# A planned start: ranks of the flags behind the far V products, and other landing costs in the plan

## The chip, the cores and the metric

One core of a Trainium2 chip runs the whole kernel in one launch. The metric is the device time in microseconds, the median of several runs.

## The reference

The reference is causal attention over 4 batches, 8 heads, 768 positions and 64 channels, and then a two-layer map over all 3072 tokens. Some heads see all earlier positions ("retrieval" heads, by a flag per head that is an input), the others see the first 4 positions ("sinks") and a window of 64:

```python
scores = scale * np.matmul(q, k.transpose(0, 1, 3, 2))
mask = np.where(retr[0, :, 0, 0, None, None], causal, causal & (is_sink | in_win))
scores = np.where(mask, scores, -1e9)
a = np.exp(scores - max); a = a / (a.sum(-1) + 1e-09)
x = np.matmul(a, v)  # (B, S, H * D) = (3072, 512)
h = x @ w_in         # 512 -> 2048
out = (h - np.tanh(h)) @ w_out   # 2048 -> 512
```

## The kernel before

The 3072 tokens are 12 tiles of 256 (three to a batch). For each tile the kernel makes Q and K with the channels in the partitions (`QK`), takes scores for each pair of heads (`st_S`, matmuls of line 1063, exp of line 1076), multiplies the probabilities with V (`st_A`, line 1156), divides (`rinv`, line 1176), lays the result out for the next matmul (`x`, line 1203, `xT`, lines 951 and 1238) and runs the two layers: H units (line 1267, tanh of line 1279, `gt` of line 1286) and O groups (line 1325, out through line 1299).

Nothing is ordered by a loop alone. Each piece of work is an `op` of the class `Plan`: an engine, a cost in ns, the keys that it reads and writes, and a priority, which is its place in the program. `Plan.run` walks through time with these costs, gives each engine the ready op of lowest priority, and so writes out each engine's order; the instructions are then issued in that order. Keys are names for the plan: real data dependencies get their semaphores from the tiles, and a key that stands for no data only delays an op in the plan.

For a DMA the plan has a cost on the issuing engine, a number of packets, ns for each packet (a sixteenth of their product is the transfer), and a pair `lag`: time from the issue to the transfer's start and from its end to the landing. Transfers of one ring go one after the other; rings that are live share. On POOL at most 8 DMAs may be under way: the ninth waits, in the plan, for the first to be done (its end + 1.8 us), the tenth for the second, and so on; if another op of POOL is ready meanwhile, it goes first. An op marked `port` on DVE that the plan starts while POOL computes, or 0.35 us or more into a DMA issue on POOL, is stretched to that op's end.

At the start, Q and K of tile 0 are loaded on SP's queue. POOL's queue brings the rest: V of tile 0 in two blocks (`load_v`, line 490), Q and K of tile 1 packed (`t16p`, line 523), V of tile 1, w_in in four parts, w_out in four parts, V, Q and K of tile 2, and tile 3's raw Q, K and V (line 592). DVE casts `t16p` into order (`in_order`, line 542), PE turns it (line 968) and DVE copies it to `QK` (line 951). `scale_v` on POOL makes the far V products `vf` (line 725): V of key blocks 0 to 3 of batch 0, times the head's flag; each tile brings two blocks. `select` (line 736) makes the mask pieces `A4` and `mS`, and one copy (line 933) fills the last part of `mS`.

From batch 1 on, heads are taken in the order of their flags. `by_rank` computes that order from the flags by a chain of small DVE instructions (lines 841 to 908), then the masks `m4r` and `mS` (lines 917 to 933), and loads the ranks `perm_i` into registers of POOL and DVE (line 938); POOL's `gather` (line 636) of tile 3 uses them. The chain's instructions wait in the plan for the keys of `LATE`.

PE's idle stretches of the first 18 us are filled, as far as the plan sees them, with products of a matrix of ones (line 1482).

Of the kernel before, what the change touches and what calls it, by code (L numbers as in the profile page):

```python
# [12 lines left out]
TT = 256  # L13
# [242 lines left out]
def kernel(  # L256
# [90 lines left out]
    XE = ("DDDD", "DDDD")  # L347
    NAMED = {"A": "ACT", "D": "DVE"}
    SV = "POOL"
    FILLS = 30  # L350
    FILL_END = 18000.0
    CASTS = (('ACT', 'DVE'), ('DVE', 'ACT'))
# [1 line left out]
    GATE = {3: (1, 0), 4: (1, 1)}  # L354
    CUT1 = (-10.5,-6.0,2.25,13.5)
    FLEX = 2
    LEAD = 3
    QUART = 7
    LD = 22
# [1 line left out]
    FROM = 3  # L361
    BR = 1
    FRONT = "A40"
    LATE = [("x16", 3)]
    BEHIND = [("x16", 1)]
    MASKS = 2
    A2 = (4, 9)
    ORDER = ("t1", "v1", 0, 1, 2, 3, 4, "t2", 5, "r3", 6, 7)

    def program(first):  # L370

# [111 lines left out]
        def load_v(t):  # L483

            b, g = divmod(t, NG)
            for i in range(NB):
                blk = g * NB + i
                dma(
                    "POOL", 900,
                    lambda i=i, blk=blk: nc.gpsimd.dma_start(  # L490
                        out=v1s[b]()[:, blk, :, 0:D],
                        in_=v[b, :, blk * 128 : blk * 128 + 128, :].rearrange("h p d -> p h d"),
                    ),
                    128 * H, 15.5, w=[("v1", b, blk, x) for x in range(2)],
                )

        def load_cast(t):

            b, g = divmod(t, NG)
            batch(b)  # L500
            c, ic = t16s[t] = buf("t16")
            if t >= FROM:
                c5 = lambda: c()[:].rearrange("p (i x h d) -> p i x h d", i=NB, x=2, h=H)
                for i in range(NB):
                    s0 = g * TT + i * 128
                    for x, src in enumerate((q, k)):
                        dma(
                            "POOL", 900,
                            lambda i=i, x=x, src=src, s0=s0: nc.gpsimd.dma_start(
                                out=c5()[:, i, x, :, :],  # L510
                                in_=src[b, :, s0 : s0 + 128, :].rearrange("h p d -> p h d"),
                            ),
                            128 * H, 15.5, w=[("t16", ic, x, i, s_) for s_ in range(H)],
                        )
                load_v(t)
                for i in range(NB):
                    turn(t, i)
                return
            packed[t] = pk, ip = buf("t16p")
            for x, src in enumerate((q, k)):  # L520
                dma(
                    "POOL", 950,
                    lambda x=x, src=src: nc.gpsimd.dma_start(
                        out=pk()[:].rearrange("p (x h e) -> p x h e", x=2, h=H)[:, x, :, :],
                        in_=src[b, :, g * TT : (g + 1) * TT, :].rearrange(
                            "h (p i) d -> p h (i d)", i=2
                        ),
                    ),
                    128 * H, 22.6, w=[("t16p", ip, x)],
                )  # L530
            if t == 1 and first:
                return
            in_order(t)
            load_v(t)

        def in_order(t):

            (pk, ip), (c, ic) = packed[t], t16s[t]
            for x in range(2):
                op(  # L540
                    "DVE", 500,
                    lambda x=x: nc.vector.tensor_copy(
                        out=c()[:].rearrange("p (x i h d) -> p x i h d", x=2, i=2, h=H)[:, x],
                        in_=pk()[:].rearrange("p (x h i d) -> p x i h d", x=2, h=H, i=2)[:, x],
                    ),
                    r=[("t16p", ip, x)] + (BEHIND if t == 1 and first else []),
                    w=[("t16", ic, x, half) for half in range(2)], port=True,
                )

        def turn(t, i):  # L550

# [166 lines left out]
        def scale_v(t, eng="POOL"):  # L718
            b, g = divmod(t, NG)
            lo = g * NB  # L720
            for jb in range(lo, min(lo + NB, 4)):
                fl = rflag0 if jb == 0 else rflag
                op(
                    eng, {"DVE": 690, "POOL": 1053}[eng],
                    lambda jb=jb, fl=fl: engs[eng].tensor_mul(
                        out=vfs[b]()[:, jb, :, :], in0=v1s[b]()[:, jb, :, :],
                        in1=fl[:].unsqueeze(2).to_broadcast([128, H, D + 1]),
                    ),
                    r=[("v1", b, jb, 0), ("v1", b, jb, 1), "rflag0", "rflag"],
                    w=[("vf", b, jb, 0)], port=True,  # L730
                )

        def select(m, src, fill, base, step, mult, key, cmp=ALU.is_ge):
# [272 lines left out]

        def st_S(units):

            todo, reads, keys, ns = [], [], [], 160
            for n, gi in units:  # L1010
                t, hp = divmod(n, HP)
                b, g = divmod(t, NG)
# [329 lines left out]
        def visits(t):  # L1342
            g = t % NG
            gen = [t * HP + hp for hp in range(HP) if not is_near(t * HP + hp)]
            near = [t * HP + hp for hp in range(HP) if is_near(t * HP + hp)]
            if near:
                a, c = gen
                d, e = near
                return {
                    0: [[(a, 0), (d, 0)], [(c, 0), (e, 0)]],  # L1350
                    1: [[(a, 0), (a, 1)], [(d, 0), (c, 0)], [(c, 1), (e, 0)]],
                    2: [[(a, 0), (a, 1)], [(a, 2), (d, 0)], [(c, 0), (c, 1)], [(c, 2), (e, 0)]],
                }[g]
# [153 lines left out]
        def spread_over(fs, lo, hi):  # L1507
            for i, f in enumerate(fs):
                plan.setdefault(max(0, int(lo + (hi - lo) * i / max(len(fs), 1))), []).append(f)

        if first and fast:
            spread_over([by_rank], BR, BR)
        spread_over(att_pairs(1) + [lambda: scale_v(1, SV)], 0, 0)
        spread_over(attention(2), *A2)
        between = {}

# [115 lines left out]
```

## Time and profile before

| | us |
|---|---|
| median of 3 runs | 232.07 |
| lowest, highest | 231.43, 232.75 |
| profiled execution, its time | 233.06 |
| profiled execution, span of its instructions | 231.3 |
| PE busy in the span | 221.7 (96%) |
| DVE, ACT, POOL busy | 146.7, 139.9, 97.5 |

The time of an execution stands beside the span that the profiler saw on the core; what lies around the span is 1.8 us here. Rows of a timeline give start, duration, engine, line, operation, output and inputs, and in brackets how long the engine was idle before and what released it. Rows of a table by stretches give for each engine the busy time and the number of instructions, then the granted PE clock (1.00 is full), the DMA share and GB/s. Rows of waits give the total, the count and the longest.

### The profile page before, as it was taken

The page shows a single profiled execution, that of the slowest core. Times are in us where ns is not written, and L with a number is a line of the kernel's source. Part 1 is how long each engine was busy: PE and PEld are TensorE (multiplying, and loading weights), DVE is VectorE, ACT ScalarE, POOL GpSimd, SP SyncE. Part 2 cuts the span into 40 slices and gives each one's busy share as a digit, 9 for nine tenths or more (in the row PEclk, how much of TensorE's full clock was granted, in tenths as well). Part 3 has the DMA queues.
Part 4 walks back from the last instruction along what each step waited for, and adds up shares of the span by engine and source line. Part 5 has one row for each costly group of instructions (what it writes and reads, how often), then busy time and mean ns, then how long its engine had stood idle before and what let it go on. Part 6 is the DMA issues. An engine that isn't in the chain of part 4 may idle for free.

```text
span 231.3 us, 6135 instructions
## 1 busy us (share of the span) xinstructions
PE 221.7 (96%) x2328; PEld 158.7 (69%) x2328; DVE 146.7 (63%) x355; ACT 139.9 (60%) x214; POOL 97.5 (42%) x231
## 2 busy tenths in 40 slices
PE   7879999989999999999999999999999999999992
PEld 6446788768887666766776676765957767766652
DVE  5878887893774766755774776466867547534400
ACT  3817837975566858747547756846875867534420
POOL 8998361980281918684363968280000000000000
PEclk9988999999999999999999999999999999999999
DMA  6999999979999999999979999944121211220112
GB/s 171 150 194 206 186 223 217 208 114 204 198 202 233 195 197 233 206 198 209 248 149 252 222 250 185 212 117 114 48 45 48 60 34 45 67 47 28 48 63 80
DMA packets 102964, 35.31 MB, mean 153 GB/s; under 512 B 90642, under 2 KB 100114, under 8 KB 102930
## 3 DMA queue, kind: packets, MB, share of 16 engines
q1 hardware_dynamic: 85632, 27.14, 56.3%
q0 software_dynamic: 17152, 7.60, 25.1%
q8 instruction: 19, 0.31, 0.6%
q14 instruction: 15, 0.12, 0.2%
q10 hardware_dynamic: 146, 0.13, 0.2%
HBM read 27.26 MB, written 6.29 MB: 145 GB/s over the span
## 4 chain that ended last, share of the span: by engine, by line
PE 84%; DVE 6%; DMA 3%; POOL 2%; ACT 2%; issue 1%; POOLq 0%; DVEq 0%
PE banks L1325 36%; PE banks L1267 34%; PE banks L1063 7%; PE banks L1156 6%; DMA t16p<-in_k_dram 3%; DVE gt L1286 2%; DVE pt L1117 2%; ACT pt L1076 1%; DVE prod L846 1%; POOL v L490 1%; PE banks L968 1%; PE banks L1052 1%; ACT th L1279 1%; DVE QK L951 0%; POOL A L736 0%
## 5 line engine op out<-in xcount | busy, mean ns | idle before, releaser
L1267 PE MATMUL banks<-xT,win 128*128 128x256 f16 x768 | 95.0, 273 | 0.7 <-DVE gt L1286 0.5
L1325 PE MATMUL banks<-wout,gt 128*128 128x512 f16 (+1 forms) x464 | 94.5, 343 | 1.1 <-DVE gt L1286 1.1
L1286 DVE SCALAR_TENSOR_TENSOR gt<-th,banks 128x512 f16<-128x512 f32 x96 | 65.1, 682 | 31.5 <-ACT th L1279 30.7
L1267 PEld LDWEIGHTS <-win 128*128 128x128 f16 x768 | 72.8, 98 | 15.5 <-issue 2.1
L1279 ACT ACTIVATE th<-banks 128x512 f32<-128x512 f32 x96 | 57.1, 601 | 40.5 <-PE banks L1267 39.4
L1076 ACT ACTIVATE pt<-banks 128x768 f16<-128x768 f32 (+1 forms) x60 | 52.9, 920 | 17.3 <-PE banks L1063 16.4
L1325 PEld LDWEIGHTS <-gt 128*128 128x128 f16 x464 | 43.0, 98 | 29.3 <-DVE gt L1286 1.3
L636 POOL CAST t<-rawqk 128x256 f16 x72 | 28.6, 443 | 30.6 <-DMA rawqk<-in_k_dram 14.7
L1299 ACT ACTIVATE ot<-banks 128x512 f32<-128x512 f32 (+1 forms) x28 | 15.0, 535 | 22.0 <-PE banks L1325 21.2
L1188 DVE TENSOR_TENSOR x16t<-banks,rinv 128x128 f32 (+1 forms) x80 | 22.9, 288 | 1.8 <-DVE x16t L1188 0.2
L1099 DVE TENSOR_TENSOR ptn<-ptn,mS 128x512 f16<-128x512 f16 x24 | 10.9, 493 | 17.0 <-ACT ptn L1076 17.0
L1063 PE MATMUL banks<-QK 64*128 64x128 f16 (+1 forms) x364 | 21.4, 241 | 0.0
L672 POOL CAST v<-rawv 128x128 f16 x72 | 19.7, 320 | 0.0
L1063 PEld LDWEIGHTS <-QK 64*128 64x128 f16 x364 | 12.7, 95 | 9.9 <-issue 6.8
L1076 ACT ACTIVATE ptn<-banks 128x1024 f16<-128x1024 f32 (+1 forms) x18 | 17.2, 953 | 3.8 <-PE banks L1063 3.7
L1156 PEld LDWEIGHTS <-pt 128*128 128x128 f16 x420 | 16.3, 97 | 3.8 <-ACT pt L1076 0.7
L1156 PE MATMUL banks<-v,pt 128*128 128x65 f16 x220 | 16.6, 193 | 0.3 <-ACT pt L1076 0.2
L1127 DVE TENSOR_TENSOR pt<-pt,m4r 128x1024 f16<-128x1024 f16 (+1 forms) x18 | 12.4, 686 | 5.0 <-ACT pt L1076 5.0
L1176 DVE RECIPROCAL rinv<-banks 128x4 f32<-128x4 f32 x48 | 8.5, 177 | 8.5 <-PE banks L1156 7.7
L1156 PE MATMUL banks<-vf,pt 128*128 128x65 f16 x200 | 13.1, 193 | 0.0
L661 POOL COPY kc<-QK 128x128 f16<-128x128 f16 x12 | 3.5, 290 | 12.0 <-DMA QK<-t 11.9
L1156 PEld LDWEIGHTS <-ptn 128*128 128x128 f16 x132 | 6.4, 97 | 2.2
(79 smaller groups left out, 137.2 us busy)
## 6 DMA issues: line engine op xcount, KB each, us to landing
out_dram<-ot SPq DMA_DIRECT2D x19, 256.0 KB, 2.5
rawqk<-in_q_dram SPq DMA_DIRECT2D x18, 256.0 KB, 3.8
rawqk<-in_k_dram SPq DMA_DIRECT2D x18, 256.0 KB, 4.4
rawv<-in_v_dram SPq DMA_DIRECT2D x16, 256.0 KB, 4.6
win<-in_moe_w_in_dram POOLq DMA_DIRECT2D x4, 512.0 KB, 11.3
wout<-in_moe_w_out_dram POOLq DMA_DIRECT2D x4, 512.0 KB, 13.2
out_dram<-ot SPq DMA_DIRECT2D x9, 128.0 KB, 3.8
v<-in_v_dram POOLq DMA_DIRECT2D x6, 128.0 KB, 6.8
```

The lines of the kernel that those rows point to most:

```text
L636: nc.gpsimd.tensor_copy(out=c5()[:, :, :, s_ : s_ + 1, :], in_=r5()[:, :, :, at, :])
L672: nc.gpsimd.tensor_copy(out=v1s[b]()[:, g * NB : g * NB + NB, RANK[s_] : RANK[s_] + 1, 0:D], in_=rv()[:, :, at, :],)
L1063: nc.tensor.matmul(out=sc()[:, hh, o : o + nb * 128], lhsT=lhsT, rhs=QK[p_, hp, q_0 : q_0 + nb * 128], start=not added, stop=not added or ...
L1076: lambda pt=pt, sc=sc, gi=gi, wid=wid: nc.scalar.activation(out=pt()[:, :, 512 * gi : 512 * gi + wid], in_=sc()[:, :, 0:wid], func=AF.Exp, ...
L1127: nc.vector.tensor_mul(out=pv, in0=pv, in1=m)
L1156: nc.tensor.matmul(out=av()[:, i, hh, :], lhsT=pt()[:, hh, co : co + 128], rhs=vv, start=(jb == first_jb), stop=(jb == qb),)
L1188: nc.vector.tensor_mul(out=xt()[:, :, at, :], in0=av()[:, :, hh : hh + 1, 0:D], in1=rinv()[:, :, hh : hh + 1].unsqueeze(3).to_broadcast([1 ...
L1267: nc.tensor.matmul(out=ph()[:, j, :], lhsT=w_in_t[fb // 4][:, cb, f0 : f0 + 128], rhs=xT()[:, :, cb, :], start=(cb == 0), stop=(cb == HP - 1),
L1279: lambda: nc.scalar.activation(out=th()[:], in_=ph()[:], func=AF.Tanh, scale=1.0 / XS),
L1286: lambda: nc.vector.scalar_tensor_tensor(out=gt()[:, u * FU : (u + 1) * FU, :], in0=th()[:], scalar=-XS, in1=ph()[:], op0=ALU.mult, op1=AL ...
L1299: nc.scalar.activation(out=ot()[:, c0:c1], in_=po()[:, c0:c1], func=AF.Copy, scale=1.0 / XS)
L1325: nc.tensor.matmul(out=po()[:, c0:c1], lhsT=gt()[:, f, ts * 128 : ts * 128 + 128], rhs=w_out_t[:, f, c0:c1], start=(f == 0), stop=(f == NF ...
```

## The change

The ranks wait in the plan for the key ("vf", 0, 3, 0), which is the product of V's key block 3 of batch 0, in place of ("x16", 3), which is the fourth head pair of tile 0's attention output. The plan's numbers of the first loads change: ns for each packet of V of tiles 0 and 1 (15.5 to 17.5), of Q of tile 1 (22.6 to 37.0), the lag of the first V load (1100 to 1500), and the fixed part of a score visit's cost on PE (160 to 225). The other edits add choices that are set to what was there: `PARTS` 1, `TRI` empty, `SPLIT` beyond every slot, `SV1` equal to `SV`, and in `scale_v` a branch for ACT that is not taken.

```diff
--- before.py
+++ after.py
@@ -347,6 +347,7 @@
     XE = ("DDDD", "DDDD")
     NAMED = {"A": "ACT", "D": "DVE"}
     SV = "POOL"
+    SV1 = "POOL"
     FILLS = 30
     FILL_END = 18000.0
     CASTS = (('ACT', 'DVE'), ('DVE', 'ACT'))
@@ -354,6 +355,12 @@
     GATE = {3: (1, 0), 4: (1, 1)}
     CUT1 = (-10.5,-6.0,2.25,13.5)
     FLEX = 2
+    V1E = 17.5
+    V0LAG = 1500
+    Q1E = 37.0
+    PARTS = 1
+    TRI = ()
+    SPLIT = 1 << 30
     LEAD = 3
     QUART = 7
     LD = 22
@@ -361,11 +368,11 @@
     FROM = 3
     BR = 1
     FRONT = "A40"
-    LATE = [("x16", 3)]
+    LATE = [("vf",0,3,0)]
     BEHIND = [("x16", 1)]
     MASKS = 2
     A2 = (4, 9)
-    ORDER = ("t1", "v1", 0, 1, 2, 3, 4, "t2", 5, "r3", 6, 7)
+    ORDER = ("t1","v1",0,1,2,3,4,"t2",5,"r3",6,7)
 
     def program(first):
 
@@ -491,7 +498,9 @@
                         out=v1s[b]()[:, blk, :, 0:D],
                         in_=v[b, :, blk * 128 : blk * 128 + 128, :].rearrange("h p d -> p h d"),
                     ),
-                    128 * H, 15.5, w=[("v1", b, blk, x) for x in range(2)],
+                    128 * H, 15.5 if t > 1 or not first else V1E,
+                    w=[("v1", b, blk, x) for x in range(2)],
+                    lag=(V0LAG, 1500) if first and blk == 0 else (1100, 1500),
                 )
 
         def load_cast(t):
@@ -517,17 +526,22 @@
                     turn(t, i)
                 return
             packed[t] = pk, ip = buf("t16p")
-            for x, src in enumerate((q, k)):
-                dma(
-                    "POOL", 950,
-                    lambda x=x, src=src: nc.gpsimd.dma_start(
-                        out=pk()[:].rearrange("p (x h e) -> p x h e", x=2, h=H)[:, x, :, :],
-                        in_=src[b, :, g * TT : (g + 1) * TT, :].rearrange(
-                            "h (p i) d -> p h (i d)", i=2
+            parts = PARTS if t == 1 and first else 1
+            n = H // parts
+            for part in range(parts):
+                hs = slice(part * n, part * n + n)
+                for x, src in enumerate((q, k)):
+                    dma(
+                        "POOL", 950 if parts == 1 else 780,
+                        lambda x=x, src=src, hs=hs: nc.gpsimd.dma_start(
+                            out=pk()[:].rearrange("p (x h e) -> p x h e", x=2, h=H)[:, x, hs, :],
+                            in_=src[b, hs, g * TT : (g + 1) * TT, :].rearrange(
+                                "h (p i) d -> p h (i d)", i=2
+                            ),
                         ),
-                    ),
-                    128 * H, 22.6, w=[("t16p", ip, x)],
-                )
+                        128 * n, Q1E if first and t == 1 and x + part == 0 else 22.6,
+                        w=[("t16p", ip, x, half) for half in ((0, 1) if parts == 1 else (part,))],
+                    )
             if t == 1 and first:
                 return
             in_order(t)
@@ -536,16 +550,26 @@
         def in_order(t):
 
             (pk, ip), (c, ic) = packed[t], t16s[t]
-            for x in range(2):
-                op(
-                    "DVE", 500,
-                    lambda x=x: nc.vector.tensor_copy(
-                        out=c()[:].rearrange("p (x i h d) -> p x i h d", x=2, i=2, h=H)[:, x],
-                        in_=pk()[:].rearrange("p (x h i d) -> p x i h d", x=2, h=H, i=2)[:, x],
-                    ),
-                    r=[("t16p", ip, x)] + (BEHIND if t == 1 and first else []),
-                    w=[("t16", ic, x, half) for half in range(2)], port=True,
-                )
+            parts = PARTS if t == 1 and first else 1
+            n = H // parts
+            for part in range(parts):
+                hs = slice(part * n, part * n + n)
+                halves = (0, 1) if parts == 1 else (part,)
+                for x in range(2):
+                    op(
+                        "DVE", 500 if parts == 1 else 290,
+                        lambda x=x, hs=hs: nc.vector.tensor_copy(
+                            out=c()[:].rearrange("p (x i h d) -> p x i h d", x=2, i=2, h=H)[
+                                :, x, :, hs, :
+                            ],
+                            in_=pk()[:].rearrange("p (x h i d) -> p x i h d", x=2, h=H, i=2)[
+                                :, x, :, hs, :
+                            ],
+                        ),
+                        r=[("t16p", ip, x, half) for half in halves]
+                        + (BEHIND if t == 1 and first else []),
+                        w=[("t16", ic, x, half) for half in halves], port=True,
+                    )
 
         def turn(t, i):
 
@@ -720,14 +744,26 @@
             lo = g * NB
             for jb in range(lo, min(lo + NB, 4)):
                 fl = rflag0 if jb == 0 else rflag
+                r = [("v1", b, jb, 0), ("v1", b, jb, 1), "rflag0", "rflag"]
...
                 op(
                     eng, {"DVE": 690, "POOL": 1053}[eng],
                     lambda jb=jb, fl=fl: engs[eng].tensor_mul(
                         out=vfs[b]()[:, jb, :, :], in0=v1s[b]()[:, jb, :, :],
                         in1=fl[:].unsqueeze(2).to_broadcast([128, H, D + 1]),
                     ),
-                    r=[("v1", b, jb, 0), ("v1", b, jb, 1), "rflag0", "rflag"],
-                    w=[("vf", b, jb, 0)], port=True,
+                    r=r, w=[("vf", b, jb, 0)], port=True,
                 )
 
         def select(m, src, fill, base, step, mult, key, cmp=ALU.is_ge):
@@ -1006,7 +1042,7 @@
 
         def st_S(units):
 
-            todo, reads, keys, ns = [], [], [], 160
+            todo, reads, keys, ns = [], [], [], 225
             for n, gi in units:
                 t, hp = divmod(n, HP)
                 b, g = divmod(t, NG)
@@ -1346,6 +1382,12 @@
             if near:
                 a, c = gen
                 d, e = near
+                if t in TRI:
+                    return {
+                        0: [[(a, 0), (d, 0), (c, 0)], [(e, 0)]],
+                        1: [[(a, 0), (a, 1), (d, 0)], [(c, 0), (c, 1), (e, 0)]],
+                        2: [[(a, 0), (a, 1), (a, 2)], [(d, 0), (c, 0), (c, 1)], [(c, 2), (e, 0)]],
+                    }[g]
                 return {
                     0: [[(a, 0), (d, 0)], [(c, 0), (e, 0)]],
                     1: [[(a, 0), (a, 1)], [(d, 0), (c, 0)], [(c, 1), (e, 0)]],
@@ -1510,7 +1552,7 @@
 
         if first and fast:
             spread_over([by_rank], BR, BR)
-        spread_over(att_pairs(1) + [lambda: scale_v(1, SV)], 0, 0)
+        spread_over(att_pairs(1) + [lambda: scale_v(1, SV1)], 0, 0)
         spread_over(attention(2), *A2)
         between = {}
 
@@ -1556,7 +1598,7 @@
                 spread_over(attention(t), lo, hi)
 
         for s, what in enumerate(slots):
-            if first and fast and s == point(2 * NG * FLEX - LEAD - 1):
+            if first and fast and s == min(SPLIT, point(2 * NG * FLEX - LEAD - 1)):
                 P.split = len(P.ops)
             fs = plan.get(s, [])
             mid = (len(fs) + 1) // 2
```

More of the change, by code (lines that the diff above doesn't have):

```diff
@@ L722, in scale_v, with fn @@
                 fl = rflag0 if jb == 0 else rflag
+                r = [("v1", b, jb, 0), ("v1", b, jb, 1), "rflag0", "rflag"]
+                if eng == "ACT":
+                    for h0 in range(0, H, 2):
+                        def fn(jb=jb, fl=fl, h0=h0):
+                            for h in (h0, h0 + 1):
+                                nc.scalar.activation(
+                                    out=vfs[b]()[:, jb, h, :], in_=v1s[b]()[:, jb, h, :],
+                                    func=AF.Copy, scale=fl[:, h : h + 1],
+                                )
+                        op("ACT", 400, fn, r=r, w=[("vf", b, jb, 0)])
+                    continue
                 op(
```

## The prediction

> **What bounds the kernel now.** I read the page's totals first, then the busy time by stretches (cut where the granted clock turns), the chain of waits, PE's waits, and the order of time on each engine between 9 and 28 us.
>
> ```profile
> PE 221.7 (96%) x2328; PEld 158.7 (69%) x2328; DVE 146.7 (63%) x355; ACT 139.9 (60%) x214; POOL 97.5 (42%) x231
> PE   7879999989999999999999999999999999999992
> PEclk9988999999999999999999999999999999999999
> ```
>
> ```profile
> core 0: us, PE busy (x) PEld busy (x) DVE busy (x) ACT busy (x) POOL busy (x), PEclk, DMA share, GB/s
> 8.40:11.80 3.40, 3.06 (x43) 1.59 (x41) 2.06 (x6) 3.40 (x8) 3.40 (x5) 1.00 1.75 160
> 11.80:15.20 3.40, 1.89 (x30) 1.32 (x28) 2.61 (x11) 0.49 (x1) 3.35 (x6) 1.00 1.71 189
> 15.20:18.66 3.46, 3.46 (x26) 1.95 (x25) 2.51 (x9) 1.44 (x2) 3.44 (x4) 0.51 1.24 206
> 18.66:22.08 3.42, 2.88 (x40) 2.05 (x38) 3.39 (x5) 2.43 (x5) 3.28 (x4) 1.00 1.24 207
> 50.00:55.00 5.00, 4.02 (x56) 3.33 (x57) 2.90 (x8) 3.08 (x5) 1.07 (x4) 1.00 0.85 171
> 62.00:216.88 154.88, 154.88 (x1566) 108.95 (x1565) 97.40 (x223) 98.16 (x147) 59.09 (x162) 1.00 0.72 148
> ```
>
> PE is the bound: from 62 to 216.88 us it is busy in all of the stretch, so nothing can be won there by another engine. What PE lacks lies early: 1.51 us idle in 11.80 to 15.20 (3.40 less 1.89), half a clock in 15.20 to 18.66 (3.46 x 0.49 = 1.70 us of work not done), 0.54 in 18.66 to 22.08, 0.98 in 50 to 55. Whatever moves the first 22 us moves the end by the same time, since PE is full behind it.
>
> ```profile
> 5.54 0.92 POOL t16p L523
> 6.46 6.11 DMA t16p<-in_k_dram
> 12.73 0.41 issue
> 13.14 0.47 DVE xT L951 x2
> ...
> 15.73 0.85 PE banks L1052 x2
> ...
> 18.80 2.39 DVE prod L846
> 21.43 0.60 DVE gt L1286
> 22.08 1.47 PE banks L1267 x12
> ```
>
> ```profile
> PE banks L1325 <- DVE gt L1286: 1.1, 1, 1.1
> PE banks L968 <- DVE t L542: 0.9, 1, 0.9
> PE banks L1267 <- DVE gt L1286: 0.5, 1, 0.5
> ```
>
> The chain shows two things that the edit touches: K of tile 1 lands and DVE then casts it in order (L542), and one tiny product of the rank computation (`prod`, L846) holds DVE for 2.4 us.
>
> ```profile
> 10.30 0.42 DVE L1203 TENSOR_TENSOR x<-banks,rinv 128x256 f16<-128x256 f32 x1
> 10.92 0.68 DVE L542 COPY t<-t16p 128x1024 f16<-128x1024 f16 x1 [0.20 <-DMA t16p<-in_q_dram]
> 12.59 0.63 DVE L542 COPY t<-t16p 128x1024 f16<-128x1024 f16 x1 [0.99 <-DMA t16p<-in_k_dram]
> 13.14 0.47 DVE L951 COPY xT<-banks 128x256 f16<-128x256 f16 x2
> 13.63 0.58 DVE L933 COPY mS<-mS 128x128 f16<-128x128 f16 x1
> 14.17 0.42 DVE L951 COPY QK<-banks 128x256 f16<-128x256 f16 x1
> 14.48 0.41 DVE L1203 TENSOR_TENSOR x<-banks,rinv 128x256 f16<-128x256 f32 x1
> 18.69 2.49 DVE L846 TENSOR_TENSOR prod<-upto,rflag 128x64 f32<-128x64 f32 x1
> 23.31 0.21 DVE L875 TENSOR_TENSOR prod<-pos_b,iota 128x64 f32<-128x64 f32 x1
> 25.68 0.14 DVE L890 TENSOR_SCALAR perm_i<-pos_a 128x8 int32<-128x8 f32 x1
> ```
>
> ```profile
> 11.63 0.36 PE L1156 MATMUL banks<-v,pt 128*128 128x65 f16 x6
> ```
>
> ```profile
> 9.09 3.00 POOL L603 DMA_DIRECT2D win<-in_moe_w_in_dram  x4
> 12.03 0.95 POOL L614 DMA_DIRECT2D wout<-in_moe_w_out_dram  x1
> 13.03 0.34 POOL L736 TENSOR_SCALAR_AFFINE_SELECT mS<-ones 64x128 f16<-64x128 f16 x1
> 15.10 1.09 POOL L725 TENSOR_TENSOR vf<-v,rflag 128x520 f16<-128x520 f16 x1
> 17.06 1.07 POOL L725 TENSOR_TENSOR vf<-v,rflag 128x520 f16<-128x520 f16 x1
> 19.02 2.07 POOL L725 TENSOR_TENSOR vf<-v,rflag 128x520 f16<-128x520 f16 x2
> 27.54 0.89 POOL L592 DMA_DIRECT2D rawqk<-in_k_dram  x1 [3.60 <-DVE m4r L917]
> ```
>
> The same shape takes 0.21 us at 23.31 and 2.49 at 18.69. The difference is POOL: its two far V products run back to back from 19.02 to 21.09 and DVE's product ends right behind them, without getting in between.
>
> **Part 1, the ranks wait for V.** The new key is ("vf",0,3,0): batch 0, key block 3, written by the second product of tile 1's `scale_v`. It is a wait in the plan alone (no data passes), so it moves some 25 DVE instructions of `by_rank` in DVE's queue and adds no semaphore. It takes `prod` out from under the products: 2.49 - 0.21 = 2.28 us of DVE. Of that only the 0.54 us is on the path, as PE waited for gt at 22.08 that long; all else of DVE's delay lay beside PE work: **-0.5 us**. Behind it on POOL's queue stands the register load of `perm_i`: POOL sat 3.60 us for it, with tile 3's loads queued behind. From the end of `prod` (21.18) to `perm_i` (25.68) are 4.5 us; a chain that starts behind the products, at about 20 to 21 us, and has the same work between, gives perm at 25 to 26. So tile 3's loads move by -0.5 to +0.5, and PE is fed by other tiles then: taken as 0.
>
> **Part 2, the landing costs.** These are the plan's own numbers and only set an order. Let T be the plan's start of the first V issue. POOL issues ten DMAs by T + 4x0.84 + 2x0.89 + 4x0.72 = T+8.02 (costs less the 0.06 overlap). The eleventh may go once the third has landed. Before: T + 0.9 + 1.1 + 2x0.992 + 1.446 + 1.8 = T+7.2: no wait. After: T + 0.9 + 1.5 + 2x1.12 + 2.368 + 1.8 = T+8.8. So in the plan POOL now has 0.8 us free there and takes what is ready: the select of mS, then the first V product. The twelfth needs K of tile 1, now T+10.25, while POOL comes free at 8.02 + 0.24 + 0.99 + 0.84 = T+10.1: it takes the second V product. Two products that stood at 15.10 and 17.06 thus move ahead of wout's first load and of V and Q, K of tile 2.
>
> DVE's order follows. Q is now due at T+8.5, but mS's select is done at T+8.3, so the mS copy goes ahead of Q's cast; the plan holds DVE through the product, by when the two xT copies and a reciprocal are ready, and they go ahead too. K's cast comes behind tile 0's third x and fourth reciprocal. That order fits the landings (Q at 10.92, K at 12.57) better: xT, rinv and x fill what was 0.99 us of waiting.
>
> Now on the chip. POOL ends the win issues at 12.09; select 0.34 and product 1.09 bring 13.4; wout 0.95 brings 14.3; the second product 1.07 brings 15.4. DVE does the mS copy (0.58) and the xT copies (0.47) from 10.72 on and the reciprocal behind the attention product that ends at 11.99; so Q's cast is next at about 12.1: a tie with POOL's select. If POOL has it, Q's cast stands until 13.4 and ends at 13.9; x (0.42) and a reciprocal bring 14.3, and K's cast ties with the second product. If DVE wins there, K ends at 14.7; if not, at 15.8. Behind K's cast there are now fewer steps to the first scores of tile 1: transposes, x 0.41, two QK copies of 0.42, some 1.3 us, where before it was 15.73 - 13.22 = 2.5. So the scores start at 16.0 or at 17.1, against 15.7: +0.3 or +1.4. If Q's cast wins its tie the first product ends at 13.9, K at 14.4, and the scores start where they did. I take **+1.0**, nearer to the blocked row, since `prod` stood through three POOL instructions without getting in; bounds 0 and +1.4.
>
> The Trainium skill (SBUF — State Buffer, § SBUF: two separate sides) says that the pair of ports is a lock held for the whole instruction by whichever starts first. By that rule each tie goes wholly one way: 0 or +1.4, never between; the 2.49 us row agrees that the loser stands.
>
> **Part 3, the cost of a score visit** goes from 160 to 225 ns + columns in the plan. It changes orders later on. Where PE is full (62 to 216.88) an order can only lose, short of 0.2 us gaps in the chain: 0 to +0.5, taken **+0.1**. The new branches with PARTS 1, an empty TRI, a SPLIT beyond every slot and SV1 on POOL leave their code as it was.
>
> **The clock.** It was halved for 3.46 us behind a stretch of 3.4 us in which PE was busy 1.89. The new order leaves PE idle later, but the plan fills known idle with `ones` products, more of them now. I take the loss as unchanged: **0**, between -1.7 (no halving) and +1.7 (a second such stretch).
>
> **Sum:** -0.5 + 1.0 + 0.1 + 0 = **+0.6 us**. The profiled execution took 233.06 (span 231.3), 0.99 above the median of 232.07; it would take 233.7, and the median 232.7.
>
> **Rivals.** *Slower: a second half-clock stretch.* Both casts blocked (+1.4), and PE's work in 15.20 to 18.66 then is transposes until 17.1 and scores after. If that doesn't count as busy the clock stays halved to 22.08: 3.42 x 0.49 = +1.7. Sum -0.5 + 1.4 + 0.1 + 1.7 = +2.7: 234.8; it decides when the scores start past about 16.9, half of that stretch. For it: 1.89 of 3.40 was not enough. Against: 3.06 was, and more fills run. The Trainium skill (TensorE: Matmul & The Clock Gate, § Part 4: PE-mode transpose) says that transposes don't count as PE-busy in the same way, which favours this rival; no row here separates them.
> *Faster: the clock stays up.* The fills and tile 0's products carry 11.80 to 15.20; then -1.7 with +0.4 for the start and -0.5: -1.8, 230.3.
> *Faster still: nothing is blocked and the wait for K is filled.* The scores start 1.0 us earlier, no halving, no `prod`: -1.0 - 1.7 - 0.5 = -3.2, 228.9. Against it stand the two products in the way.
> *It does nothing:* the order on POOL stays because real limits set it. Against: the order is written out at build time; with part 1 alone it would be 231.6.
>
> **Chances.** A measurement of this kernel can tell about 0.5%, 1.16 us, from no change. The forecast's case 0.42 (its bounds run from -0.5 to +1.6: 0.33 same, 0.09 slower); second half-clock stretch 0.27 (all slower); clock stays up 0.18 (0.15 faster, 0.03 same); nothing blocked 0.08 (faster); part 1 alone 0.05 (0.04 same, 0.01 faster). Faster 0.24, same 0.40, slower 0.36. The range reaches from the clock that stays up, 230.3, to the second stretch, 234.8; it leaves out the 0.08 below and some of the ends. The forecast's own case runs from 231.6 to 233.7.
>
> **What would show it.** Part 1: `prod` L846 at about 0.2 us, behind the last L725, and no PE wait for gt near 22 us. Part 2: two L725 products between 12 and 16 us, ahead of L614; L542 casts of over 0.7 us, or starting late though their data has landed; the first L1052 of tile 1 between 15.7 and 17.2. Clock: the half-clock stretch once, 3.4 us long. The forecast is wrong if the L1052 of tile 1 starts before 15 us, if there is no or a second stretch of half clock, or if PE idles again behind 62 us.

## The result, and the profile after

| | median of 8 runs | lowest to highest | profiled execution (span) |
|---|---|---|---|
| before | 231.92 us | 231.43 to 233.49 | 233.06 (231.3) |
| after | 233.88 us | 233.65 to 234.55 | 233.69 (231.9) |

The ratio of the runs, after to before, is 1.0075 with a 95% interval of 1.0053 to 1.0097. The medians lie 1.96 us apart; taken from the ratio, by which this text goes, the change costs 1.75 us (1.2 to 2.25). Forecast were +0.6, a range from 230.3 to 234.8 and a chance of 0.36 for slower by over 0.5%. The two profiled executions lie only 0.6 us apart, because the one of before was 1.1 us above its own median. So the pair shows well what was reordered and what stands where, but not where all of the 1.75 us arise; for that the experiments are needed.

The page of after, totals and slices:

```profile
PE 220.9 (95%) x2350; PEld 159.0 (69%) x2350; DVE 145.9 (63%) x355; ACT 139.8 (60%) x214; POOL 96.9 (42%) x231
PE   6859999989999999999999999999999999999992
PEclk9999999999999999999999999999999999999998
```

The busy time by stretches, cut as before:

```profile
core 0: us, PE busy (x) PEld busy (x) DVE busy (x) ACT busy (x) POOL busy (x), PEclk, DMA share, GB/s
11.80:15.20 3.40, 1.55 (x30) 1.21 (x27) 3.40 (x4) 0.49 (x1) 3.33 (x5) 1.00 1.70 187
15.20:18.66 3.46, 2.53 (x39) 1.94 (x40) 3.46 (x12) 0.32 (x1) 2.93 (x5) 1.00 1.24 205
18.66:22.08 3.42, 2.98 (x33) 2.10 (x30) 3.37 (x13) 2.60 (x4) 3.42 (x4) 1.00 1.25 207
62.00:216.88 154.88, 154.49 (x1561) 108.47 (x1559) 95.51 (x221) 97.89 (x147) 58.02 (x162) 1.00 0.70 147
```

DVE is busy in all of 11.80 to 15.20, but with 4 instructions where it did 11 before. PE idles 1.85 us there and 0.93 in the next stretch, and the clock was not halved in this execution (1.00 in all of these stretches). Behind 62 us PE lacks 0.39 us that it didn't lack before. The order of time on DVE (start, duration, line, output and input):

```profile
10.65 0.18 DVE L969 COPY mS<-mS 128x128 f16<-128x128 f16 x1
11.70 0.49 DVE L987 COPY xT<-banks 128x256 f16<-128x256 f16 x2 [0.86 <-PE banks L1274]
12.10 0.17 DVE L1212 RECIPROCAL rinv<-banks 128x4 f32<-128x4 f32 x1
12.19 3.55 DVE L561 COPY t<-t16p 128x1024 f16<-128x1024 f16 x1
15.66 0.41 DVE L1239 TENSOR_TENSOR x<-banks,rinv 128x256 f16<-128x256 f32 x1
16.09 0.45 DVE L561 COPY t<-t16p 128x1024 f16<-128x1024 f16 x1
17.86 2.09 DVE L987 COPY QK<-banks 128x256 f16<-128x256 f16 x6
19.96 0.80 DVE L882 TENSOR_TENSOR prod<-upto,rflag 128x64 f32<-128x64 f32 x1
```

and on POOL:

```profile
12.14 0.28 POOL L772 TENSOR_SCALAR_AFFINE_SELECT mS<-ones 64x128 f16<-64x128 f16 x1
12.41 1.04 POOL L762 TENSOR_TENSOR vf<-v,rflag 128x520 f16<-128x520 f16 x1
13.41 0.95 POOL L638 DMA_DIRECT2D wout<-in_moe_w_out_dram  x1
14.38 1.07 POOL L762 TENSOR_TENSOR vf<-v,rflag 128x520 f16<-128x520 f16 x1
15.38 0.94 POOL L497 DMA_DIRECT2D v<-in_v_dram  x1
18.59 2.08 POOL L762 TENSOR_TENSOR vf<-v,rflag 128x520 f16<-128x520 f16 x2
```

Both orders are the ones that the prediction worked out, but for mS's copy, which was done early. Q's cast (L561, 12.19) starts 0.05 us behind POOL's select and then stood not only through select and product, but through wout's issue and the second product as well: its 3.55 us end at 15.74, behind the product's end at 15.45. The same cast of K, when POOL does no product, takes 0.45. PE's waits in after show that it waits for what is queued behind the cast, a third x (in us: total, times, longest):

```profile
PE banks L1274 <- DVE x L1239: 2.8, 1, 2.8
PE banks L1361 <- DVE gt L1322: 1.0, 2, 0.7
PE banks L1004 <- DVE t L987: 0.7, 1, 0.7
PE banks L1303 <- DVE QK L987: 0.4, 1, 0.4
```

The order of time on PE in after, and below it in before, shows what that delays:

```profile
17.32 0.59 PE L1088 MATMUL banks<-m,ident 128*128 128x512 f16 x2
19.34 1.91 PE L1303 MATMUL banks<-xT,win 128*128 128x256 f16 x16 [0.44 <-DVE QK L987]
```

```profile
15.52 1.06 PE L1052 MATMUL banks<-m,ident 128*128 128x512 f16 x2
17.78 2.30 PE L1267 MATMUL banks<-xT,win 128*128 128x256 f16 x16
```

The first row of each is the first scores of tile 1, which begin 1.80 us later, and the second the first unit of the expert layer (xT times `win`, called H below), which begins 1.56 us later.

### The profile page after: what moved, and what is told of

Its sections match the earlier page's. It is cut to its first block, busy times and chain, and to the rows that moved or that the text cites. A ratio compares the mean times of both kernels' runs of the same rounds, so it can differ in the third digit from the quotient of the medians.

```text
span 231.9 us, 6182 instructions
## 1 busy us (share of the span) xinstructions
PE 220.9 (95%) x2350; PEld 159.0 (69%) x2350; DVE 145.9 (63%) x355; ACT 139.8 (60%) x214; POOL 96.9 (42%) x231
## 4 chain that ended last, share of the span: by engine, by line
PE 89%; DVE 7%; ACT 2%; issue 0%; POOL 0%; POOLq 0%
PE banks L1303 36%; PE banks L1361 35%; PE banks L1099 8%; PE banks L1192 7%; DVE t L561 2%; DVE gt L1322 1%; DVE pt L1153 1%; PE banks L1524 1%; PE banks L1088 1%; DVE QK L987 1%; PE banks L1004 1%; DVE m L862 1%; ACT pt L1112 1%; ACT QK L985 1%; DVE x L1239 0%
## 5 line engine op out<-in xcount | busy, mean ns | idle before, releaser
L660 POOL CAST t<-rawqk 128x256 f16 x72 | 27.6, 431 | 28.5 <-DMA rawqk<-in_k_dram 15.8
L1099 PE MATMUL banks<-QK 64*128 64x128 f16 (+1 forms) x364 | 21.0, 238 | 0.0
L1135 DVE TENSOR_TENSOR ptn<-ptn,mS 128x512 f16<-128x512 f16 x24 | 10.1, 459 | 16.8 <-ACT ptn L1112 16.8
L1112 ACT ACTIVATE ptn<-banks 128x1024 f16<-128x1024 f32 (+1 forms) x18 | 17.1, 952 | 4.6 <-PE banks L1099 4.5
L1099 PEld LDWEIGHTS <-QK 64*128 64x128 f16 x364 | 12.5, 94 | 9.2 <-issue 6.6
L685 POOL COPY kc<-QK 128x128 f16<-128x128 f16 x12 | 4.1, 343 | 13.1 <-DMA QK<-t 13.1
L1524 PE MATMUL banks<-ones 128*128 128x128 f16 x73 | 6.8, 256 | 1.4 <-POOL ones L795 1.4
```

The source lines that it names most:

```text
L660: nc.gpsimd.tensor_copy(out=c5()[:, :, :, s_ : s_ + 1, :], in_=r5()[:, :, :, at, :])
L1099: nc.tensor.matmul(out=sc()[:, hh, o : o + nb * 128], lhsT=lhsT, rhs=QK[p_, hp, q_0 : q_0 + nb * 128], start=not added, stop=not added or ...
L1112: lambda pt=pt, sc=sc, gi=gi, wid=wid: nc.scalar.activation(out=pt()[:, :, 512 * gi : 512 * gi + wid], in_=sc()[:, :, 0:wid], func=AF.Exp, ...
```

## The experiments

The kernels ran in three groups on three chips, each group beside its own runs of the kernel before (medians 233.38 of 29 runs, 233.41 of 29, 233.35 of 27). Times compare only within a group, so the ratios to before are what counts. The row of after is the pair of runs above, with a kernel before of its own (231.92), so a comparison with it is one of ratios from different groups. All edits are to the kernel after. First the list, in the order of the ratio, with the start of tile 1's scores and of H in each profile:

| kernel | scores | H | ratio (95%) |
|---|---|---|---|
| only_ranks | 15.78 | 18.04 | 0.9993 (0.9969 to 1.0017) |
| before | 15.52 | 17.78 | 1 |
| q31 | 15.67 | 17.48 | 1.0013 (0.9979 to 1.0047) |
| held_products | 14.29 | 17.35 | 1.0022 (1.0003 to 1.0041) |
| casts_on_act | 15.53 | 17.59 | 1.0031 (1.0002 to 1.0060) |
| win_early_act | 17.16 | 16.31 | 1.0036 (1.0005 to 1.0067) |
| q28 | 17.06 | 19.20 | 1.0037 (1.0008 to 1.0066) |
| win_early_after | 17.35 | 19.20 | 1.0039 (1.0015 to 1.0063) |
| only_landings | 16.80 | 18.85 | 1.0043 (1.0018 to 1.0069) |
| after | 17.32 | 19.34 | 1.0075 (1.0053 to 1.0097) |
| win_early | 18.12 | 19.98 | 1.0078 (1.0047 to 1.0110) |
| only_visit | 15.32 | 17.66 | 1.0117 (1.0086 to 1.0147) |
| visit_ot4 | 15.33 | 17.11 | 1.0117 (1.0069 to 1.0164) |
| ranks_landings | 18.33 | 20.42 | 1.0121 (1.0085 to 1.0157) |

### One part of the change at a time

The ranks alone (landing costs and visit cost as before):

```
-    V1E = 17.5        +    V1E = 15.5
-    V0LAG = 1500      +    V0LAG = 1100
-    Q1E = 37.0        +    Q1E = 22.6
-  st_S: ns = 225      +  st_S: ns = 160
```

> The kernel before, with the ranks of the flags behind the last far V product and nothing else changed. Only DVE's order differs (27 places) and two places on POOL. Theory A (the two casts of tile 1 that stand behind far V products cost the time; the ranks alone help): prod in about 0.2 us instead of 2.49, PE's 0.5 us wait for gt near 22 us gone, 231.2 to 231.7 us against 231.9. Theory B (the score visit's cost reorders the rest and costs the time): the same here. Rival: perm comes later and tile 3's loads with it: 232.2 or more.

It measured 233.13, ratio 0.9993: -0.16 us with an interval from -0.7 to +0.4. Its row of `prod` and its third stretch (18.66 to 22.08) show what Part 1 said:

```profile
21.83 0.19 DVE L882 TENSOR_TENSOR prod<-upto,rflag 128x64 f32<-128x64 f32 x1
```

```profile
18.66:22.08 3.42, 3.42 (x47) 2.62 (x45) 2.25 (x8) 2.55 (x4) 3.40 (x4) 1.00 1.24 208
```

PE is full in the stretch in which it waited 0.54 us for gt before. What that is worth is too small to be told from nothing.

The landing costs alone:

```
-    LATE = [("vf",0,3,0)]   +    LATE = [("x16", 3)]
-  st_S: ns = 225            +  st_S: ns = 160
```

> The kernel before with the new landing numbers of V, Q and the first lag, and the ranks and the visit cost as before. Theory A: Q's cast stands for about 3.5 us again, first scores of tile 1 at about 17.3 us instead of 15.7, and the time is that of the whole change or more, 233.5 to 234.6 us. Theory B: the late start is paid back by the clock that stays up, 231.5 to 232.4 us.

It measured 234.49, ratio 1.0043. On the same order of DVE and POOL, Q's cast won its tie here, and K's cast stood in its place, from inside the first product (12.73 to 13.78) until behind the end of the second (14.70 to 15.77):

```profile
12.21 0.39 DVE L561 COPY t<-t16p 128x1024 f16<-128x1024 f16 x1
12.94 3.12 DVE L561 COPY t<-t16p 128x1024 f16<-128x1024 f16 x1
```

The cost of a visit alone:

```
-  V1E, V0LAG, Q1E as after  +  V1E, V0LAG, Q1E as before
-    LATE = [("vf",0,3,0)]   +    LATE = [("x16", 3)]
```

> The kernel before with the score visit's fixed cost at 225 ns in the plan and nothing else. Theory A: within 0.5 us of before, 231.5 to 232.5. Theory B: this edit carries the loss, 233 to 234 us, with PE idle or with short gaps behind 62 us.

It measured 236.27, ratio 1.0117: +2.7 us, the largest effect of a single part, from the part that was forecast at +0.1. The start is good (scores 15.32). Its longest wait on PE lies at 41 us, and the chain of waits shows it whole:

```profile
37.59 6.11 DMA out_dram<-ot
43.81 0.39 ACT ot L1335
44.25 3.18 PE banks L1303 x16
```

```profile
PE banks L1303 <- ACT ot L1335: 2.6, 1, 2.6
```

An eviction of an output unit (`ot`) on ACT waits for the store that reads its buffer, the store takes 6.1 us, and PE waits 2.6 us for the eviction. In the kernel before, two such evictions follow each other at 37.32 and 38.11 with no wait for a store; with the dearer visit the second eviction gets a buffer that a store still reads.

To take that wait away a fourth buffer was given:

```
-    BANKS = {..., "ot": 3, ...}   +    BANKS = {..., "ot": 4, ...}     (on only_visit)
```

> The kernel before with the visit cost at 225, and four instead of three output tiles; every engine's order is the same as with the visit cost alone. There ACT stood 2.75 us at 41 us for a store's DMA of 6.1 us and PE 2.6 us behind it. If that wait is the price of the visit cost (theory D: an accident of the order), it goes and the ratio to before falls from 1.012 to 0.999 to 1.004. If not (theory B: the later order as such), it stays above 1.008.

It measured 236.01, ratio 1.0117, and PE's wait was still there: the plan takes the lowest buffer that it believes free, and here again that was one that a store still read.

```profile
PE banks L1303 <- ACT ot L1335: 2.8, 1, 2.8
```

The run did not take the wait away, then, but its trace says that the wait is not all of the 2.7 us. The profiled execution of visit_ot4 took 234.29 with this wait in it; its median is 236.01. In only_visit PE ran at half clock right behind the wait (0.50 in each of the three microseconds from 45 to 48), in visit_ot4's profile at 1.00. The 16 matmuls of 44.25 in the chain above took 3.18 us there, and here:

```profile
43.91 1.91 PE banks L1303 x16
```

Of only_visit's six executions five have a mean clock of 0.993 or less (median 236.33), the one at 1.0 took 235.47. So a wait of 2.6 us and a half-clock stretch behind it (by estimate some 3.4 us at half, 1.7 us of work) both stand in only_visit's profile, against half a clock near 17 us in the one of before; how the 2.7 us divide was not shown.

Ranks and landings together, without the visit cost:

```
-  st_S: ns = 225      +  st_S: ns = 160
```

> The changed kernel with the score visit's cost at 160 again: ranks and landings alone. Theory A: same start as the changed kernel (Q's cast stands 3.5 us), time between landings alone (+0.4% of before) and the whole change (+0.75%). Theory B: if the visit's cost adds to it as it did alone (+1.2%), this is 0.5 to 1% faster than the changed kernel, at or below before.

It measured 236.19, ratio 1.0121. By the middle values this is 1.1 us slower than the whole change (1.0075; the intervals just overlap), though the part taken out costs 2.7 us by itself. Q's cast on DVE stands as in after, and in the two stretches behind it the clock was down for part of the time:

```profile
12.21 3.56 DVE L561 COPY t<-t16p 128x1024 f16<-128x1024 f16 x1
```

```profile
15.20:18.66 3.46, 2.50 (x22) 2.33 (x23) 2.83 (x9) 0.00 (x0) 2.93 (x5) 0.65 1.25 206
18.66:22.08 3.42, 3.42 (x36) 2.36 (x35) 2.79 (x10) 2.11 (x3) 3.42 (x4) 0.85 1.24 206
```

Both expectations for this run were missed. The clock takes part here too: of its six executions the one with a mean clock of 1.0 took 234.15, the five of 0.993 or less have a median of 236.34.

The three parts don't add: 0.9993, 1.0043 and 1.0117 would make 1.0153, and the whole is 1.0075. Each edit rewrites the written-out order, and the store that is met at 41 us in one order is not met in another.

### Is it the cast that stands?

The theory after the first group: what costs the time is DVE's SBUF copies standing while POOL multiplies. Its rivals: the new order as such, or DMAs issued later. Three edits take the products away from the casts, each in another way. The first makes the plan hold the products back until K's cast is done:

```
+                if t == 0 and first:
+                    r += [("t16", t16s[1][1], x, half) for x in range(2) for half in range(2)]
```

> The whole change, but in the plan the two far V products of tile 0 also wait for the casts of tile 1, so that they cannot stand ahead of them; everything else as in the changed kernel. Theory A: both casts take under 0.7 us, right behind their landings at 10.9 and 12.6 us, the first scores of tile 1 start by 15 us, and the time falls by 1.5 us or more against the changed kernel: 230.8 to 232.4. Theory B: it stays at 233.3 to 234.3, since the later order is as in the changed kernel.

It measured 234.01, ratio 1.0022. The casts take 0.56 and 0.86 and the scores start at 14.29, three microseconds ahead of after. Against after 1.2 us are gone, less than the 1.5 that were expected. H meets a new wait:

```profile
17.35 0.61 PE L1305 MATMUL banks<-xT,win 128*128 128x256 f16 x4 [0.61 <-DMA win<-in_moe_w_in_dram]
```

The second leaves POOL's order as it is in after and does tile 1's two casts on ACT:

```
-                        "DVE", 500 ...
-                        lambda ...: nc.vector.tensor_copy(
+                        "ACT" if t == 1 and first else "DVE",
+                        1030 if t == 1 and first else 500,
+                        lambda ...: (nc.scalar.copy if t == 1 and first else nc.vector.tensor_copy)(
```

> The changed kernel, with the two casts of tile 1 (L561) on ACT in place of DVE; the far V products stand where they stand in the changed kernel, ahead of w_out and tile 2. If the casts stood because DVE and POOL exclude each other (theory A), ACT's casts take about 1 us each and are done by about 14.4 us with the products beside them, and the first scores of tile 1 start at 15.3 to 16 us instead of 17.3; the time falls by 0.7 to 1.5 us against the changed kernel. If the data itself was late (rival), the casts on ACT end no earlier than 15.5. If the start of the H units is set by the landing of w_in near 17.5 us (theory C), the scores come earlier and the time falls by under 0.7 us.

It measured 233.63, ratio 1.0031. ACT's cast runs 13.17 to 14.25 beside the end of the product and is no longer than the other:

```profile
11.53 1.08 ACT L562 COPY t<-t16p 128x1024 f16<-128x1024 f16 x1
13.17 1.08 ACT L562 COPY t<-t16p 128x1024 f16<-128x1024 f16 x1
```

```profile
12.50 1.04 POOL L766 TENSOR_TENSOR vf<-v,rflag 128x520 f16<-128x520 f16 x1
```

The two rows above are ACT's, the last is POOL's. H again waits for `win`, 0.53 us before it begins at 17.59. So the data of the casts was there, and the standing is DVE's beside POOL. That POOL's product doesn't hold ACT is seen over 0.5 us only (12.50 to 12.61 and 13.17 to 13.54). The third sets the plan's landing of tile 1's Q, and with it K's, between before and after, which leaves one product in the way, not two:

```
-    Q1E = 37.0        +    Q1E = 31.0     (q31)        +    Q1E = 28.0     (q28)
```

> The changed kernel with 31 instead of 37 ns for each packet of tile 1's Q: in the plan the first product still goes ahead of w_out, the second no longer, and Q's cast goes ahead of the product. Theory A: Q's cast near 11 us under 0.8 us, K's cast stands for one product (done by about 13.9); first scores of tile 1 at 15 to 16 us; 0.3 to 1.2 us faster than the changed kernel. Theory B: within 0.5 us of it.

> The changed kernel with 28 instead of 37 ns for each packet of tile 1's Q. The release of the eleventh POOL DMA then comes just before the select of mS ends in the plan, so that w_out goes first and a product behind it. Theory A: one product between Q's cast and K's, Q's cast under 0.8 us near 11 us, K's cast stands about 1 us; first scores of tile 1 at 15.5 to 16.5; 0.3 to 1 us faster than the changed kernel. Theory B (later order decides): as the changed kernel, 0 to 0.5 us either way.

q31 measured 233.45 (ratio 1.0013), q28 234.06 (1.0037). In both, Q's cast is done ahead of the product and K's cast meets one; q28 also has a half-clock stretch at 17 us. Its scores start at 17.06, later than expected and 1.39 us behind q31's; its K cast is done 1.02 us behind q31's. K's cast in q31, then in q28:

```profile
12.61 1.16 DVE L561 COPY t<-t16p 128x1024 f16<-128x1024 f16 x1 [0.32 <-DMA t16p<-in_k_dram]
```

```profile
12.81 1.98 DVE L561 COPY t<-t16p 128x1024 f16<-128x1024 f16 x1 [0.44 <-DMA t16p<-in_k_dram]
```

Against after's 1.0075 (1.0053 to 1.0097), held_products and q31 lie below with intervals that don't touch, and casts_on_act with one that overlaps by 0.0007: without a cast that stands for over 3 us, 1.0 to 1.4 of the 1.75 us are gone. That size is not firm. A cast stands for 3.12 us in only_landings (1.0043) and in win_early_after, below (1.0039), and neither can be told from casts_on_act. All four kernels in which a cast stands for over 3 us are at 1.0039 or more, and those without, leaving aside win_early and the two with the visit cost alone, at 1.0037 or less. So the standing cast costs time in after's order, but how much of the 1.75 us is the new order as such is not settled. What is left, 0.3 to 0.7 us by the middle values, was not traced to one wait: in held_products PE idles 2.66 us between 22.08 and 62 us, where before has 1.32; in casts_on_act PE idles 1.32 us between 62 and 140 us and in q31 1.65, where PE waits for a transfer of K or Q (`PE banks L1099 <- DMA QK<-t: 1.3, 1, 1.3` in q31), but how much of that reaches the end was not tried.

### What would be next: the load of win

When the scores are early, H waits for `win`. So with `win`'s loads ahead of V's the fast start should be worth something:

```
-    ORDER = ("t1","v1",0,1,2,3,4,"t2",5,"r3",6,7)
+    ORDER = ("t1",0,"v1",1,2,3,4,"t2",5,"r3",6,7)
```

This was done on only_ranks (win_early), on after (win_early_after), and on only_ranks with the casts on ACT (win_early_act).

> The kernel before with the ranks behind the far V products, and the first part of w_in issued ahead of V of tile 1; no other edit. Theory C (the landing of w_in near 17.5 us sets the start of the H units, so an earlier start of the scores buys little): the first H unit starts before 17.4 us, waiting for xT and not for w_in, and the time falls by 0.3 to 1 us against before. Theory A (the casts set the start): H starts as before at about 17.8, time within 0.3 us of the kernel with the ranks alone.

> The whole change, with the first part of w_in issued ahead of V of tile 1. The casts stand behind the products as in the changed kernel. Theory A: H starts at 19 to 19.5 us as in the changed kernel, no gain: ratio to before 1.005 to 1.01. Theory C (w_in): H starts 0.5 us or more earlier than 19.3, 0.5 us gained.

> As win_early, with the two casts of tile 1 on ACT: nothing of tile 1's start stands behind a POOL product or a POOL issue. Theory C: the best start of all, H before 17 us, 231.5 to 233 us on a chip where before has 233.4. Theory A alone: as the ranks alone, within 0.5 us of before.

They measured 234.98 (1.0078), 234.21 (1.0039) and 234.36 (1.0036). For win_early neither expectation came true (H at 19.98). POOL's two products came together, behind an issue of V, and another SBUF copy stood: that of mS, 0.18 us in after. All nine of its executions have a mean clock of 0.993 or less, so its 1.8 us are not the copy's alone. DVE's row first, then POOL's:

```profile
13.64 2.75 DVE L969 COPY mS<-mS 128x128 f16<-128x128 f16 x1
```

```profile
13.34 0.90 POOL L497 DMA_DIRECT2D v<-in_v_dram  x1
14.26 2.07 POOL L762 TENSOR_TENSOR vf<-v,rflag 128x520 f16<-128x520 f16 x2
```

In win_early_act no copy stood and H began at 16.31, 1.5 us ahead of before, and the kernel was still not faster than before: its scores came behind H, and PE waited 1.7 us in all for gt and 1.6 for pt. In that order an earlier H bought nothing. (The profiled execution was at 0.52 of the clock from 15.20 to 18.66; nine others with a mean clock of 0.998 or more have a median of 234.12, no faster than before either.) In win_early_after, `win` first is no remedy either: K's cast stands and H begins at 19.20.

## Why the prediction was right or wrong

**The orders: right.** The landing costs put mS's select and the first far V product ahead of wout's issue and the second ahead of V's; DVE does mS and xT, a reciprocal and then Q's cast; the tie at about 12.1 was one (in after the cast came at 12.19 and the select at 12.14; in only_landings 12.21 and 12.26). In win_early_after the select's row starts first, 12.17 against 12.20, and the cast still goes through (0.40, the select 0.57), so rows this close don't say who wins. The first product stands ahead of wout's issue and the second behind it, as the working has it; "two L725 products ... ahead of L614" among its signs does not fit that working.

**The price of the lost tie: mis-sized, and that is the step which failed.** The prediction let Q's cast in at wout's issue, between the products: done at 13.9, scores at 16.0 or 17.1, +1.0 taken, +1.4 at most. Measured is a cast that ends at 15.74, scores at 17.32 and H 1.56 us late. The row that points this way was named in the prediction: in before, `prod` starts at 18.69 inside an issue (18.06 to 19.0) that stands directly ahead of a product, and didn't get in. It was used only to lean towards the blocked branch, whose price still let the cast in. Nor is the other branch what was priced: in only_landings Q's cast won its tie, for which the prediction had 0, and K's cast then stood for 3.12 us. That only_landings measured +1.0, the number taken for this part, is luck. In the list above a later H goes through to the end about one to one: only_landings +1.07 us of H and +1.0 us of time, after +1.56 and +1.75, win_early +2.2 and +1.8, ranks_landings +2.64 and +2.8; q28 and win_early_after, with +1.42 and +0.9, lie under it. This is a likeness between one profile and a median in each, not a test, and where H is early the time does not follow (held_products, the two with the visit cost).

The rule of the Trainium skill that was weighed (SBUF — State Buffer, § SBUF: two separate sides: the pair of ports is held by whichever starts first, for the whole instruction) agrees with a tie that goes wholly one way, 0.39 against 3.55 us. Taken for the products alone, it would have let the cast in at 13.4, when the first product ended; the measured hold went on through the issue between the two products, so here the measurement decides.

**Part 1, -0.5: right in mechanism, not measurable.** In after `prod` took 0.80 rather than 0.21, as it starts at 19.96 inside the last products; in only_ranks it took 0.19 and the wait for gt is gone, for -0.16 us (-0.7 to +0.4).

**Part 3, +0.1 with 0.5 at most: wrong alone, masked in the sum.** It argued from where PE is full, behind 62 us. Alone the edit costs 2.7 us, with a wait of 2.6 us at 41 to 44 us and half a clock behind it, where the prediction did not look. Beside the other two parts the same edit goes with a ratio that is lower than without it.

**The clock, -1.7 to +1.7: wrong price for the kernel before.** After had no half-clock stretch in its profile, though the prediction counted on one, and yet was slower. A stretch of 3.46 us at 0.51 takes 0.007 from the mean clock over 231 us, so an execution whose mean is under 0.9945 is taken here as one with such a stretch. By this five of after's eight executions had one; their median is 233.90, that of the other three 233.69. The kernel before ran both ways on all three chips: on the first, 8 runs under 0.9945 have a median of 233.14 us, 13 runs of 0.9985 and more have 233.56; on the second chip it is 233.46 (6 runs) and 233.40 (17), on the third 232.88 (9) and 233.39 (8). A half clock of 3.46 us costs nothing that can be seen there. The likely reason is that H would have waited for `win` at full clock: held_products, casts_on_act, q31, only_visit and visit_ot4 have their scores early and start H at 17.11 to 17.66 with a wait of 0.3 to 0.9 us for that load, and before starts it at 17.78. In other orders it does seem to cost: q28's eight executions under 0.9945 have a median of 234.23, its four others 232.92, and only_visit and ranks_landings are slower with it too, as said above. So the slower rival had the right sign for another reason in after, and "the clock stays up" came true in its profile and brought nothing.

**Faster still, 228.9: held back by the load of `win`**, which the prediction didn't look for: it never asked what H needs beside the scores. held_products does what this rival wanted (nothing stands, scores 1.2 us ahead of before) and is at 1.0022; beside the wait for `win` it has the longer idle times of PE up to 62 us named above.

**The range: luck in part.** The measured 233.88 lies above the end of the forecast's own case (233.7). Inside the range it stands by the room left for the second half-clock stretch, which after's profile doesn't have. Of the prediction's own signs, three speak against it: no half-clock stretch, the scores at 17.32 rather than between 15.7 and 17.2, and 0.39 us of idle PE behind 62 us. With the upper bounds of parts 2 and 3 its own case adds up to +1.4 (-0.5 + 1.4 + 0.5), not to the +1.6 that it gives.

## What to carry to other kernels

Before a reorder is costed, lay the SBUF-to-SBUF instructions of DVE beside POOL's vector instructions in order of time: a copy of 0.4 us that met two products on POOL with one issue between them lasted 3.1 to 3.6 here, and what was queued behind it came late. A gain at the start is worth at most the distance to the next bound, so look for the load that the next stage waits on before counting it. In an order that is written out by a planner, a changed cost is a new draw of the whole order: try its parts singly, and don't add them.

## What the hardware showed that was not expected

None of the f16 copies of the start got in on DVE during a single DMA issue on POOL that stood directly ahead of a product: after (issue 13.41 to 14.36, cast done at 15.74), only_landings (13.73 to 14.68, done at 16.06), q28 (12.50 to 13.41, done at 14.79), win_early (13.34 to 14.24, done at 16.39). One did when another issue followed: q31's cast was done at 13.77, 0.29 us behind the end of its product. The plainest pair is the copy of mS: in before it starts at 13.63 inside the issue of V (13.32 to 14.22), another issue follows, and it takes 0.58 and ends with that issue; in win_early it starts at 13.64 inside the same issue, the products follow, and it takes 2.75.

The small product `prod` keeps to no such rule. In before it stands through a single issue and the two products behind it (18.69, 2.49 us); in visit_ot4 the same instructions stand in the same order on POOL (issue 18.09 to 19.03, products from 19.05), and `prod`, which starts in the product ahead of them, is done at 18.58, inside the issue:

```profile
17.61 0.97 DVE L882 TENSOR_TENSOR prod<-upto,rflag 128x64 f32<-128x64 f32 x1
```

In casts_on_act it takes 0.22 us from 17.62, in the second of two issues and directly ahead of two products. What decides whether DVE gets in is open.

What stood were DVE's instructions with all inputs in SBUF. In after the six copies out of PSUM (`QK<-banks`, 2.09 us for six from 17.86) run into POOL's products of 18.59 to 20.67 at 0.35 us each, no longer than the two before them (0.77 for both from 17.00), while `prod`, from SBUF, stands from 19.96 to 20.76. Not every one of them stood: the reduction that follows the copies (`iota`) has its input in SBUF too and took 0.20 us from 19.84, beside the products.
